# A third buffer for V's global rows, and new written-out orders for all five engines

## The chip, the cores and the metric

The kernel runs on one core of a Trainium2 chip. The time is device microseconds of one execution on that core. Three runs of the kernel before gave 323.43, 324.93 and 328.83 us; their median is 324.93 us.

## The reference

```python
def _attn_ref(q_l, k_l, v_l, q_g, k_g, v_g):          # l: 8 x 8 x 512 x 64, g: 8 x 8 x 32 x 64
    k_all = np.concatenate([k_g, k_l], axis=2); v_all = np.concatenate([v_g, v_l], axis=2)
    out_g = np.matmul(sm(scale * np.matmul(q_g, k_all.T)), v_all)           # global rows see all
    s_ll = np.where(np.abs(pos[:, None] - pos[None, :]) <= 32, scale * q_l @ k_l.T, -1e9)
    s_l = np.concatenate([scale * q_l @ k_g.T, s_ll], axis=-1)              # local rows: 32 global keys and a band
    out_l = np.matmul(sm(s_l), np.concatenate([v_g, v_l], axis=2))
    return np.concatenate([out_g, out_l], axis=2)

def _moe_ref(x, w_in, w_out):                         # x: 4352 x 512, d_ff 2048
    h = x @ w_in
    return (h * np.clip(h + 3.0, 0.0, 6.0) / 6.0) @ w_out
```

Eight batches of eight heads go through a banded attention with 32 global rows; its output, one row of 512 numbers per token, goes through a two-layer network with a hard-swish between the layers. Inputs and output are float32.

## The kernel before

Everything inside is float16 with float32 accumulation. A batch b is cut into four blocks j of 128 local tokens. The work of a batch comes in these steps; the words in italics are used for them below.

- *Loads.* Queries, keys and values come from DRAM in rows of one head, converted to float16 on the way, by DMAs that POOL issues (`load`, the DMA itself at L478): for each block one of queries and one of keys into a buffer `nat` (eight of them, L362), five pieces of values into `ve` (three buffers, one per batch in turn, L366) and the global rows of queries and keys into `natg`. Four small loads per batch put V's global rows, once more, into `vgz` (two buffers before the change, L368): a layout with zeros in which four pairs of heads take 32 rows each (`load_vg`, L559).
- *Turns.* Queries and keys are transposed into `qk`, on TensorE for the first three batches, by DMA transposes that SP issues (L616) for the later ones.
- *Strips.* Two DMAs of SP (L585) copy the values, shifted by half a block, into `st`. They need all five pieces of values of their batch.
- *Score* of (b, j), L676: the products of 64 queries with 128 keys in the band and with the global keys; then the softmax, on VectorE (L701) and ScalarE (L712), and its scaling into `pn` (L731, L737).
- *Turned* (b, j): the weights `pn` transposed into `et`, on TensorE for two batches, later by a DMA transpose of SP (L760).
- *The product with the values* of (b, j): L771 for the global rows out of `vgz`, L776 for the band out of `ve` and `st`. From the seventh block on (`JOIN`, L803) it is emitted together with the score of the block two places later: one operation of TensorE does the score of (2, 2), for instance, and then the value product of (2, 0).
- *Global rows*: their scores (L825), softmax, the transposes (L867 by DMA) and the product with the values (L884, called *gav* below).
- *The network*: `first` (L907, four matmuls of up to 512 columns into one PSUM bank), the activation on ScalarE (L914) and VectorE (L918), `second` (L930), the copy out of PSUM (L399 on ScalarE, L401 on VectorE) and the store by SP (L948).

Each of the five engines does its work strictly in the order of a list, `ORDER` (L16 to L121): the operations' numbers, written out. The lists also say which of ScalarE and VectorE does a copy that either could do. A planner (`Plan.lay`) runs over the lists once when the program is built and gives every operation its buffer; the DMA model in it adds `LATE` (1500 ns) to the landing of a load. When an operation at the head of an engine's list has to wait, all behind it on that engine wait too. That holds for POOL and SP, which only issue DMAs here: 160 on POOL, 114 on SP.

A load waits for what its buffer still holds: one into `nat` for the turn of an earlier block, one into `ve` for all that batch b - 3 does with its values, gav included, and one into `vgz` for the value products of batch b - 2:

```python
deps = [av_last[b - 2, j] for j in range(NJ)] if b >= 2 else [cleared(b)]
```

A DMA besides waits until the one eight places before it on its queue has landed. "Place n" below is the n-th number of an engine's list, counted from 0. Numbers of operations that come up, with what they are: 496 is the last piece of V of batch 2, 497 to 500 are the four vgz loads of batch 2, 735 and 736 the queries and keys of block (3, 0), 985 and 986 those of (4, 3), 1242 the last piece of V of batch 5, 1487 the second piece of V of batch 6; 594 is turned (2, 2), 755 and 756 the turns of (3, 0) and (3, 1), 1008 the turn of (4, 3), 1035 turned (4, 0); 16 is the load of the 32 keys after the first block (the halo, L522).

## Time and profile before

| | |
|---|---|
| three runs | 323.43, 324.93, 328.83 us |
| profiled execution | 326.44 us, of which 324.6 us are the span from first to last instruction |
| busy: TensorE, VectorE, ScalarE, POOL | 307.8, 269.7, 226.2, 121.6 us |
| granted TensorE clock | 1.000 |
| DMA | 46.35 MB in 178864 packets, 169345 of them under 512 B |

Busy time of POOL is the time of issuing DMAs. In the tables of waits an engine's idle time is put down to the instruction after it and to what released that. A DMA's "landing" is counted from its issue to the semaphore that tells of its data. SP's instructions stand as "SPq": they are its queue's own, and their duration is that of the issue, not of the transfer.

### The profile page before, as it was taken

What the parts mean: (1) busy time and instruction counts of PE and PEld (TensorE: products, weight loads), DVE (VectorE), ACT (ScalarE), POOL (GpSimd) and SP (SyncE); (2) the same over time, 40 slices, a digit from 0 to 9 for tenths busy, and PEclk for the clock granted to TensorE, in tenths of its full rate; (3) what the DMA queues carried; (4) which work ended last, traced back from release to release, by engine and by line L of the source; (5) the groups of instructions that cost most, each with busy time, mean ns of one, the idle gap of its engine ahead of it and who ended that gap; (6) DMA issues with size and microseconds to landing.
All of it is one profiled execution on the core that took longest, in us unless ns stands there. A gap on an engine that the chain in (4) does not pass through costs nothing.

```text
span 324.6 us, 9722 instructions
## 1 busy us (share of the span) xinstructions
PE 307.8 (95%) x3653; PEld 174.3 (54%) x3653; DVE 269.7 (83%) x978; ACT 226.2 (70%) x742; POOL 121.6 (37%) x167
## 2 busy tenths in 40 slices
PE   7887989999998999999999779999999999999995
PEld 3566876668854544444544344445444545745543
DVE  4899999899997899799999779999988987476311
ACT  2899999998875797489767566697768664576000
POOL 7966943988820569192208610260000000000000
PEclk9999999999999999999999999999999999999999
DMA  9999999999999999999999998999746027400032
GB/s 153 155 187 177 141 206 164 142 173 142 157 175 205 186 179 158 217 206 142 177 161 182 174 128 205 154 166 146 139 107 162 19 50 107 139 0 2 24 105 98
DMA packets 178864, 46.35 MB, mean 143 GB/s; under 512 B 169345, under 2 KB 173697, under 8 KB 178817
## 3 DMA queue, kind: packets, MB, share of 16 engines
q0 software_dynamic: 108800, 17.28, 75.7%
q1 hardware_dynamic: 70016, 28.45, 47.5%
q8 instruction: 28, 0.46, 0.6%
q14 instruction: 20, 0.16, 0.2%
HBM read 35.65 MB, written 8.91 MB: 137 GB/s over the span
## 4 chain that ended last, share of the span: by engine, by line
PE 55%; DMA 22%; DVE 8%; POOL 7%; issue 3%; SPq 2%; ACT 2%; POOLq 0%; ACTq 0%
PE m L930 24%; PE m L907 23%; DMA et<-pn 9%; DMA wout<-in_moe_w_out_dram 5%; DMA nat<-in_k_l_dram 4%; POOL nat L478 3%; DVE sm L701 2%; DMA nat<-in_q_l_dram 2%; POOL ve L478 2%; SPq L616 2%; PE s L676 2%; PE s L776 2%; DVE pn L731 1%; DMA natg<-in_k_g_dram 1%; PE m L884 1%
## 5 line engine op out<-in xcount | busy, mean ns | idle before, releaser
L712 ACT ACTIVATE sm<-sm,stat 128x160 f32<-128x160 f32 x256 | 106.8, 421 | 28.6 <-DVE stat L701 28.4
L930 PE MATMUL m<-wout,gs 128*128 128x512 f16 (+1 forms) x560 | 125.7, 373 | 0.1
L907 PE MATMUL m<-xt,win 128*128 128x512 f16 (+2 forms) x704 | 119.0, 321 | 0.9 <-ACT xt L399 0.8
L918 DVE SCALAR_TENSOR_TENSOR gs<-t,m 128x512 f16<-128x512 f32 x136 | 89.5, 680 | 13.3 <-ACT t L914 12.8
L907 PEld LDWEIGHTS <-win 128*128 128x128 f16 x768 | 68.7, 98 | 48.6 <-issue 1.6
L914 ACT ACTIVATE t<-m 128x512 f32<-128x512 f32 x136 | 77.5, 594 | 24.6 <-PE m L907 22.6
L930 PEld LDWEIGHTS <-gs 128*128 128x128 f16 x560 | 52.8, 98 | 56.2 <-issue 1.6
L701 DVE CUSTOM_DVE_ANT_0 sm<-s,mask 128x160 f32<-128x160 f32 x256 | 69.1, 317 | 7.4 <-PE s L776 4.5
L712 ACT ACTIVATION_READ_ACCUMULATOR sm<-sm,stat 128x1 f32 x256 | 49.0, 192 | 0.0
L731 DVE TENSOR_TENSOR pn<-sm,stat 128x512 f16<-128x512 f32 x64 | 43.3, 685 | 0.6
L478 POOL DMA_DIRECT2D ve<-in_v_l_dram x40 | 32.7, 827 | 25.6 <-PE m L884 17.7
L478 POOL DMA_DIRECT2D nat<-in_q_l_dram x30 | 27.2, 907 | 15.2 <-DMA qk<-nat 9.9
L399 ACT COPY ot<-m 128x512 f32<-128x512 f32 (+1 forms) x22 | 12.2, 561 | 25.7 <-PE m L930 24.6
L478 POOL DMA_DIRECT2D vgz<-in_v_g_dram x28 | 15.8, 570 | 37.0 <-PE s L771 35.6
L478 POOL DMA_DIRECT2D nat<-in_k_l_dram x30 | 27.0, 905 | 5.9 <-DMA ve<-in_v_l_dram 2.7
L676 PEld LDWEIGHTS <-qk 64*64 64x64 f16 x1024 | 13.8, 107 | 15.8 <-issue 13.3
L401 DVE COPY ot<-m 128x512 f32<-128x512 f32 x13 | 9.0, 689 | 15.7 <-PE m L930 15.7
L701 DVE DVE_READ_ACCUMULATOR2_ANT stat<- 128x1 f32 x256 | 21.0, 82 | 0.0
L676 PE MATMUL s<-qk 64*64 64x128 f16 x512 | 17.1, 224 | 3.7 <-DVE stat L701 1.8
L401 DVE CAST xt<-s 128x512 f16<-128x512 f32 x26 | 17.8, 684 | 2.6 <-PE s L776 2.6
L676 PE MATMUL s<-gt,qk 64*64 64x32 f16 x512 | 14.7, 176 | 0.0
L737 DVE TENSOR_TENSOR pn<-sm,stat 128x256 f16<-128x256 f32 x32 | 13.4, 419 | 0.2
(82 smaller groups left out, 242.9 us busy)
## 6 DMA issues: line engine op xcount, KB each, us to landing
out_dram<-ot SPq DMA_DIRECT2D x31, 256.0 KB, 4.2
nat<-in_q_l_dram POOLq DMA_DIRECT2D x30, 128.0 KB, 6.4
nat<-in_k_l_dram POOLq DMA_DIRECT2D x30, 128.0 KB, 7.3
st<-ve SPq DMA_DIRECT2D x14, 256.0 KB, 4.5
ve<-in_v_l_dram POOLq DMA_DIRECT2D x24, 128.0 KB, 5.9
win<-in_moe_w_in_dram POOLq DMA_DIRECT2D x4, 512.0 KB, 8.7
wout<-in_moe_w_out_dram POOLq DMA_DIRECT2D x4, 512.0 KB, 11.4
ve<-in_v_l_dram POOLq DMA_DIRECT2D x8, 96.0 KB, 5.6
```

Of the source, the lines that this page charges most:

```text
L399: nc.scalar.copy(out=out, in_=in_)
L401: nc.vector.tensor_copy(out=out, in_=in_)
L478: nc.gpsimd.dma_start(out=dst(op), in_=src)
L676: nc.tensor.matmul(out=out[q, P:KW] if n == G else out[q, 0:P], lhsT=qk[r][rows, 0, p, UQ + j * P + u * QP:UQ + j * P + (u + 1) * QP], rhs ...
L701: nc.vector.tensor_tensor_reduce(out=sm[sm_op.slot][:, h, :], in0=head(psS[s.slot], h), in1=m, scale=-scale, scalar=3.0e38, op0=ALU.add, o ...
L712: nc.scalar.activation(out=sm[sm_op.slot][:, h, :], in_=sm[sm_op.slot][:, h, :], func=EXP, scale=-1.0, bias=stat[stat_op.slot][:, 0, h:h + 1],
L731: nc.vector.tensor_tensor(out=pn[pn_op.slot][:, h0:h1, :], in0=sm[sm_op.slot][:, h0:h1, 0:P], in1=stat[stat_op.slot][:, 2, h0:h1].unsqueez ...
L737: nc.vector.tensor_tensor(out=pn[pn_op.slot][:, H:H + 2, :].rearrange("q a (h g) -> q (a h) g", g=G), in0=sm[sm_op.slot][:, :, P:KW], in1= ...
L907: nc.tensor.matmul(out=psM[op.slot][:, i * n:(i + 1) * n], lhsT=w_in_t[:, m, (c + i) * P:(c + i + 1) * P], rhs=x()[:, m, t0:t0 + n], start ...
L914: nc.scalar.activation(out=t1[to.slot], in_=psM[f.slot], func=RELU, bias=0.5, scale=1.0 / 6.0)
L918: nc.vector.scalar_tensor_tensor(out=gs[set_.slot][:, c:c + k, t0:t0 + n], in0=t1[to.slot].rearrange("f (k t) -> f k t", k=k), scalar=1.0, ...
L930: nc.tensor.matmul(out=psM[(f or op).slot][:, a * n:(a + 1) * n], lhsT=gs[set_.slot][:, c, t0:t0 + P], rhs=w_out_t[:, c, a * n:(a + 1) * n ...
```

## The change

`vgz` becomes three buffers, used in turn; its loads wait for the value products of batch b - 3 in place of b - 2; the second clearing step sets one more buffer to zero; and all five lists of `ORDER` are replaced.

```diff
-    vgz = many(2, [P, NP, P], FP16, "vgz")
+    vgz = many(3, [P, NP, P], FP16, "vgz")
...
-            nc.vector.memset(vgz[r], 0.0)
+        for x in vgz[:1] if first else vgz[1:]:
+            nc.vector.memset(x, 0.0)
...
-    add("DVE", 1100, lambda: clear(False), key=-5.0)
+    add("DVE", 1640, lambda: clear(False), key=-5.0)
...
-        deps = [av_last[b - 2, j] for j in range(NJ)] if b >= 2 else [cleared(b)]
+        deps = [av_last[b - 3, j] for j in range(NJ)] if b >= 3 else [cleared(b)]
...
-        return [load(lambda op, k=k: vgz[b % 2]...
+        return [load(lambda op, k=k: vgz[b % 3]...
...
-    lhsT=vgz[r][...]
+    lhsT=vgz[b % 3][...]
```

TensorE's list holds the same 372 operations in both; 140 of them stand at the same place, and no block's score moves by more than a few places (the score of (2, 2) is at place 93 in both, that of (4, 2) at 170 in both). The score of (3, 0) goes from 115 to 116, gav of batch 3 from 185 to 189. Ten copies go from VectorE to ScalarE and six the other way. The lists of POOL and SP hold the same DMAs in another order. POOL's, places 37 to 161:

```diff
     "POOL": """
...
-        226 224 228 221 222 45 481 229 230 46 47 48 482 487 479 480 483 488 489 490 485 496 484 492 497 486 495
-        493 494 491 739 747 1229 745 741 987 499 737 500 498 738 988 981 742 989 735 750 736 751 752 990 1725
-        1231 743 749 744 740 1232 979 982 980 746 748 1241 983 1240 1239 995 999 993 998 984 997 994 1235 1230
-        985 1238 1236 992 1481 996 986 1479 991 1246 1243 1244 1000 1475 1727 1476 1726 1482 1237 1484 1723 1245
-        1242 1233 1234 1729 1488 1483 1492 1477 1473 1724 1728 1494 1474 1489 1487 1491 1493 1480 1730 1490 1478
-        1485 1486 1737 1736 1740 1735 1733 1731 1739 1738 1732 1734
+        227 221 222 231 47 230 229 232 45 46 48 481 482 487 490 479 480 483 488 489 484 494 485 745 486 492 495
+        737 493 491 738 735 739 741 747 742 1229 496 497 987 990 499 989 500 498 988 751 981 750 744 740 982 748
+        736 985 746 749 979 980 1725 991 743 752 1231 1242 993 983 1235 1239 1479 996 984 1238 1237 1230 995
+        1241 994 1233 1000 1236 998 1245 1481 997 992 999 1234 986 1473 1240 1232 1723 1474 1475 1476 1487 1729
+        1486 1730 1243 1244 1724 1480 1246 1727 1477 1740 1488 1737 1489 1478 1483 1482 1484 1490 1738 1732 1734
+        1493 1728 1736 1739 1494 1485 1731 1733 1726 1735 1491 1492
```

And the first lines of SP's:

```diff
     "SP": """
-        11 16 10 19 20 234 233 457 502 501 539 756 566 755 594 471 478 464 758 757 621 1006 753 754 785 734 1005
-        812 720 840 1007 867 727 713 1002 1008 1035 1001 978 964 1250 1062 876 883 1249 1090 1247 1252 1251 1117
+        11 19 10 16 20 233 234 457 539 501 502 758 478 566 755 756 594 757 1006 621 471 734 753 754 785 1005 720
+        812 840 464 1007 867 713 727 1001 1002 1008 1035 978 964 1248 1062 1250 1249 876 883 1090 1247 957 1251
```

## The prediction

> **What bounds the kernel now.** I read the page first, then the table of waits, POOL's timeline, the chain of waits, and SP's timeline beside TensorE's.

> ```profile
> PE 307.8 (95%) x3653; PEld 174.3 (54%) x3653; DVE 269.7 (83%) x978; ACT 226.2 (70%) x742; POOL 121.6 (37%) x167
> ```

> TensorE is busy for 307.8 of 324.6 us, and the change takes no matmul away. What can be won is its idle time; what can be lost is more of it. So the question about each of the other engines is only whether it lets TensorE wait.

> ```profile
> POOL vgz L478 <- PE s L771: 35.6, 3, 19.7
> ...
> POOL ve L478 <- PE m L884: 17.7, 1, 17.7
> ...
> PE s L771 <- DMA et<-pn: 3.4, 3, 2.5
> ...
> PE s L676 <- DVE stat L701: 1.8, 3, 0.8
> ```

> The columns are the total in us, the number of times and the longest. POOL stands for 35.6 us in front of loads into vgz, three times, until a value product of two batches earlier is done. That is the wait which the third buffer takes away. TensorE, however, waits only 3.4 us for transposed weights and 1.8 us for VectorE's softmax in these rows. The wait on POOL is seven times what reaches TensorE. The timeline of POOL tells where the three are, and what is queued behind each:

> ```profile
> 109.03 0.89 POOL L478 DMA_DIRECT2D ve<-in_v_l_dram  x1 [17.68 <-PE m L884]
> ...
> 136.82 2.15 POOL L478 DMA_DIRECT2D vgz<-in_v_g_dram  x4 [7.38 <-PE s L771]
> ...
> 171.45 0.54 POOL L478 DMA_DIRECT2D vgz<-in_v_g_dram  x1 [8.55 <-PE s L771]
> ...
> 209.16 0.53 POOL L478 DMA_DIRECT2D vgz<-in_v_g_dram  x1 [19.72 <-PE s L771]
> ...
> 214.21 1.71 POOL L478 DMA_DIRECT2D ve<-in_v_l_dram  x2
> ```

> ```profile
> 228.71 0.56 SPq L585 DMA_DIRECT2D st<-ve  x1
> ```

> Behind the longest of them (19.72 us) only batch 7's values and vgz rows are left; the last is issued by 215.9, and SP's copy of them into the strips starts at 228.71. A margin of 12.8 us against a landing of some 6 us (row of the vgz loads below) says that this wait costs nothing. The one that ends at 136.82 holds the vgz rows of batch 4 and loads of batches 5 to 7, none of which TensorE is seen to wait for. Only the one that ends at 171.45 stands near a stall:

> ```profile
> 159.71 0.58 PE m L884 x20
> ...
> 172.17 8.47 DMA et<-pn
> ```

> ```profile
> 180.68 0.31 PE L771 MATMUL s<-et,vgz 64*64 64x128 f16 x8 [2.53 <-DMA et<-pn]
> ...
> 188.32 0.74 PE L884 MATMUL m<-eg,ve 128*128 128x64 f16 x20 [1.68 <-DVE gs L918]
> ```

> The chain runs through the transpose of weights (5, 0) issued at 172.17, which takes 8.47 us. It was issued 0.7 us after POOL came free and began to issue a dozen loads without a pause. TensorE idles 2.53 us for it, and 1.68 us more 7 us later, when ScalarE and VectorE have to catch up. How much of the 8.47 us is POOL's doing is seen in all transposes of weights, from 60 to 200 us and after 200, when few loads are left:

> ```profile
> L760 SPq DMA_TRANSPOSE et<-pn x15: 1336/2433/3948, 70.4 to 193.7; - x15
> ...
> DMA to landing us min/median/max: 3.4/7.2/9.4
> ```

> ```profile
> L760 SPq DMA_TRANSPOSE et<-pn x9: 1255/1339/1898, 201.6 to 275.8; - x9
> ...
> DMA to landing us min/median/max: 3.4/3.4/5.0
> ```

> The same transpose lands after 7.2 us beside loads and after 3.4 us without. A load that goes out early is therefore not free: it lengthens the transpose beside it, on which TensorE's value products wait.

> **The change part by part.** The sum is made against the profiled execution: 326.44 us, span 324.6 us and 1.84 us around it. It lies 1.5 us above the median of 324.93 us of three runs from 323.43 to 328.83, so it is one ordinary run. The numbers of instructions on POOL, SP and TensorE stay what they are.

> *The clear and the halo.* One more memset of vgz:

> ```profile
> 2.59 0.27 DVE L450 MEMSET vgz<- 128x256 uint32 x1
> ...
> 6.53 0.22 DVE L401 COPY gt<-m 128x128 f16<-128x128 f16 x1 [2.16 <-PE m L641]
> ```

> It costs VectorE 0.27 us at a time after which it idles 2.16 us for TensorE; hidden, and 0.27 us if that cover were gone. On SP the halo load goes from place 1 to place 3, past the loads 19 and 10 (both of 256 KB).

> ```profile
> 1.27 0.56 SPq L522 DMA_DIRECT2D t<-in_k_l_dram  x1
> ```

> ```profile
> single<-in_q_l_dram SPq DMA_DIRECT2D x2, 256.0 KB, 5.1
> ...
> t<-in_k_l_dram SPq DMA_DIRECT2D x1, 64.0 KB, 2.7
> ```

> ```profile
> 7.48 1.08 ACT qk L399 x2
> 8.60 0.57 PE s L676 x32
> ```

> Behind two more issues like its own of 0.56 us it goes out at about 2.4. It lands at 5.1 if it takes its 2.7 us again, at 7.5 if it takes the 5.1 us of the big ones ahead of it. Then come four small transposes and a copy like that of 0.22 us above. The first score starts at 8.60 behind ScalarE's copies, which end at 8.56: that is the cover. I take 0; bounds 0 and +0.5. Copies that change between ScalarE and VectorE I take at 0: in the middle TensorE waits for none of them, and the last copy before the last store stays on ScalarE (0.37 us below is all that it could add).

> ```profile
> 321.04 0.37 ACT L399 COPY ot<-m 128x256 f32<-128x256 f32 x1 [2.66 <-PE m L930]
> ```

> *Batch 2's loads go back.* In POOL's list 496 moves from place 52 to 68 and the vgz loads 497 to 500 from 55, 70, 67 and 69 to 69, 75, 72 and 74, behind loads of batch 3. TensorE's operation that uses them keeps its place.

> ```profile
> 76.06 0.58 POOL L478 DMA_DIRECT2D natg<-in_q_g_dram  x1
> ```

> ```profile
> 79.33 0.28 PE L771 MATMUL s<-et,vgz 64*64 64x128 f16 x8
> ```

> ```profile
> L478 POOL DMA_DIRECT2D vgz<-in_v_g_dram x28: 533/552/762, 24.6 to 213.7; - x28
> ...
> DMA to landing us min/median/max: 3.3/5.9/9.9
> ```

> Place 75 was issued at 76.06 before; a vgz load there lands at 82.0 by the median, 2.6 us after its use at 79.33. But the places 68 to 75 now hold small loads that issue in some 0.55 us (the median of that row), where four were full loads of about 0.9 us (0.89 in the row at 109.03): up to 1.4 us earlier, so 1.2 us late. I take **+1.5 us**, near that end, since the eight places before it are all small now; bounds 0 (a landing after 3.3 us) and +6.6 us (after 9.9).

> *Batch 3's turns.* The keys 736 of block (3, 0) move from place 78 to 84, and turned (2, 2) now stands behind both turns of batch 3 (place 16, was 14).

> ```profile
> 78.27 6.16 DMA nat<-in_k_l_dram
> ```

> ```profile
> 82.55 0.62 POOL L478 DMA_DIRECT2D ve<-in_v_g_dram  x1
> ```

> ```profile
> 84.47 1.24 SPq L616 DMA_TRANSPOSE qk<-nat  x1
> ...
> 89.20 1.47 SPq L760 DMA_TRANSPOSE et<-pn  x1
> ```

> ```profile
> 96.99 0.28 PE L771 MATMUL s<-et,vgz 64*64 64x128 f16 x7
> ```

> The load at 78.27 took 6.16 us and let SP go at 84.47. At place 84 it is issued at 82.55 and lands at 88.7; two turns of 1.24 us follow, and turned (2, 2) goes out at 91.2 in place of 89.20. Its weights land 7.2 us later, at 98.4; the value product wants them at 96.99, so 1.4 us late. As TensorE is itself already up to 1.5 us behind by then, but part of this lag moves the transpose too, I take **+1.0 us**, bounds 0 and +2.5.

> *Behind the wait for gav 2.* POOL's wait of 17.68 us for ve stays where it is: place 95 (1242) wants gav of batch 2 as place 94 did. Behind it the keys 986 of block (4, 3) stand at place 119, were at 113.

> ```profile
> 127.08 0.90 POOL L478 DMA_DIRECT2D nat<-in_k_l_dram  x1
> ```

> ```profile
> 133.83 2.00 SPq L616 DMA_TRANSPOSE qk<-nat  x1
> 136.07 2.43 SPq L760 DMA_TRANSPOSE et<-pn  x1
> ```

> ```profile
> 146.40 0.28 PE L771 MATMUL s<-et,vgz 64*64 64x128 f16 x8
> ```

> From 109.03 to 127.08 are 19 places, 0.95 us each. 24 places give 131.8; the landing took 6.75 us (127.08 to 133.83), so SP's turn goes out at 138.6, turned (4, 0) 2.2 us behind it at 140.8, and its weights land at 148.0, 1.6 us after 146.40. I take **+1.3 us** since some small loads are among the 24; bounds 0 and +3.8 (a landing of 9.4 us).

> *The wait that goes, and the one that comes.* No vgz load stands any more in front of what is urgent. But 1487, a piece of V for batch 6, now stands at place 127 and wants gav of batch 3, done at 160.3. From 109.03 the 32 places before it take 30 us, so POOL comes to it at 139 and waits there for about 20 us, where it had stood for 7.38 and 8.55 us. When it is let go at 160, the loads behind it run beside the weights of (4, 2) and (4, 3) in place of (5, 0). The stall of 2.53 and 1.68 us may go; some of it comes back there. I take **-1.5 us**; bounds -4.2 and 0.

> [...]

> The sum: 326.44 + 0 + 1.5 + 1.0 + 1.3 - 1.5 = **328.7 us**, 1.2% over the median. Two per cent of it, 6.5 us, is about what a measurement of this kernel can tell from no change: 318.4 to 331.4 us.

> **The rivals.** *The stalls go and nothing comes.* The chain through 172.17 speaks for it: POOL free earlier, loads spread out, no burst beside (5, 0). TensorE gets back 2.53 + 1.68 us and the other 0.9 us of its 3.4 us for weights: 326.44 - 5.1 = 321.3 us. Against it are the ve waits, which hold POOL as long as the vgz waits did, and the places of 496 to 500. With VectorE's 1.8 us besides it would be 319.5, which is about the floor.

> *SP's line gets late in every batch: slower.* Turns and weights share SP's list, so a late load of keys holds a turn, and that holds the weights behind it. It decides where the keys at places 84 and 119 land over 6.2 and 6.75 us after their issue; from then each late us goes to TensorE. At the longest landings seen the first batch costs 6.6 us and the fourth 3.8: 326.44 + 10.4 = 336.8 us. For it: landings of 9.4 and 9.9 us are in the rows, and three value products already wait for weights. Against it: a lag of TensorE gives later loads time again.

> *A wait for a wait.* The ve wait does what the vgz wait did, moved batches cancel out: the change does not do what it says, and the time stays at 326.4 us, as the profiled run, or 325 by the median.

> **How the numbers follow.** Forecast 0.37, its own range 325.5 to 332.5; the stalls go 0.20; SP's line late 0.33; a wait for a wait 0.10. Faster by over 2% takes the lower two fifths of the second: 0.08. Slower by over 2% takes all of the third and 0.05 of the forecast: 0.38. Within 2%: 0.54. The range from 319.5 to 338 runs from the floor of the second case to just over the third's price.

> **What would show it.** Right: POOL's waits for vgz near 0 and one wait for ve of 15 to 20 us that ends near 160; a wait of TensorE for vgz or st near 79 and for et near 97 and 146; less at 178 to 188. Wrong: no wait of TensorE over 1 us between 75 and 150 (then the places of 496, 736 and 986 were priced too high), or waits for et over 2 us in several batches (then SP's line decides).

## The result, and the profile after

The kernel after takes 322.57 us (median of 22 executions, 318.55 to 328.94), the kernel before beside it on the same chip 326.86 us (22 executions, 321.81 to 331.34). The ratio is 0.9892 [0.9855, 0.993]: 1.1% faster, with the executions of the two overlapping. Ratios here are taken over those executions that lie within 1.5% of their kernel's fastest (13 of the 22 of after); the two medians alone would give 0.987. The profiled execution of after takes 322.16 us, its span 320.4 us.

First the page, engines' busy time, then the tables of waits of TensorE and POOL (total us, times, longest; lines from L451 on are one higher than before):

```profile
PE 308.5 (96%) x3658; PEld 174.4 (54%) x3658; DVE 266.4 (83%) x975; ACT 229.5 (72%) x746; POOL 121.4 (38%) x167
```

```profile
PE s L772 <- DMA et<-pn: 2.4, 3, 1.6
...
PE s L777 <- DMA st<-ve: 0.5, 1, 0.5
...
POOL ve L479 <- PE m L885: 23.3, 3, 12.2
POOL nat L479 <- DMA qk<-nat: 23.0, 4, 9.7
```

TensorE's work is the same. The 35.6 us for which POOL stood in front of loads into vgz are gone, and about half of them come back in other places: 23.3 us for gav in front of loads into ve (17.7 before) and 23.0 us for turns in front of loads into nat (9.9 before). POOL issues its last load at 194.6 us, where it was 215.9. What TensorE loses, by its timeline:

```profile
79.31 0.32 PE L777 MATMUL s<-et,st 128*64 128x64 f16 x8 [0.48 <-DMA st<-ve]
...
88.74 0.31 PE L772 MATMUL s<-et,vgz 64*64 64x128 f16 x8 [1.57 <-DMA et<-pn]
...
99.59 0.31 PE L772 MATMUL s<-et,vgz 64*64 64x128 f16 x8 [0.26 <-DMA et<-pn]
...
121.89 0.31 PE L772 MATMUL s<-et,vgz 64*64 64x128 f16 x8 [0.52 <-DMA et<-pn]
```

The chain of waits names the transfers behind the first two of these, a piece of V, the strips and turned (2,1):

```profile
69.00 6.93 DMA ve<-in_v_l_dram
...
75.96 3.22 DMA st<-ve
...
79.26 9.44 DMA et<-pn
```

There are new waits early, as the prediction had it, though only one of them is over 1 us, and none is left where the kernel before lost 2.53 and 1.68 us. TensorE's busy time in two stretches, before and then after (columns: window, its length, TensorE, its weight loads, VectorE, ScalarE, POOL, granted clock, DMA share, GB/s):

```profile
160.00:180.00 20.00, 18.12 (x239) 8.76 (x235) 18.81 (x67) 13.33 (x49) 10.30 (x14) 1.00 1.48 174
180.00:200.00 20.00, 17.64 (x192) 8.75 (x195) 15.92 (x57) 14.39 (x47) 4.98 (x7) 1.00 1.62 175
```

```profile
160.00:180.00 20.00, 19.86 (x277) 9.89 (x276) 17.61 (x65) 12.88 (x47) 14.45 (x20) 1.00 1.79 195
180.00:200.00 20.00, 20.00 (x216) 9.95 (x214) 19.81 (x76) 15.88 (x53) 10.47 (x16) 1.00 1.79 161
```

35.76 us of work in 40 before, 39.85 after: 4.1 us, nearly the whole difference of 4.3 us between the two profiled executions. It is tempting to stop here. The experiments show that the place of this gain belongs in part to these two executions and not to the kernels.

### The profile page after: what moved, and what is told of

Read it like the earlier page. It is cut to its first block, busy times and chain, and to the rows that moved or that the text cites. A ratio compares the mean times of both kernels' runs of the same rounds, so it can differ in the third digit from the quotient of the medians.

```text
span 320.4 us, 9717 instructions
## 1 busy us (share of the span) xinstructions
PE 308.5 (96%) x3658; PEld 174.4 (54%) x3658; DVE 266.4 (83%) x975; ACT 229.5 (72%) x746; POOL 121.4 (38%) x167
## 4 chain that ended last, share of the span: by engine, by line
PE 67%; DVE 15%; DMA 14%; issue 2%; ACT 1%; POOL 1%; POOLq 0%
PE m L931 33%; PE m L908 23%; DMA et<-pn 9%; DVE sm L702 4%; DVE gs L919 4%; DVE pn L732 3%; PE s L677 3%; PE s L777 3%; DMA ve<-in_v_l_dram 2%; DMA natg<-in_k_g_dram 1%; PE m L885 1%; PE s L772 1%; DMA st<-ve 1%; ACT sm L713 1%; PE m L749 1%
## 5 line engine op out<-in xcount | busy, mean ns | idle before, releaser
L479 POOL DMA_DIRECT2D ve<-in_v_l_dram x40 | 33.1, 833 | 27.1 <-PE m L885 23.3
L399 ACT COPY ot<-m 128x512 f32<-128x512 f32 (+1 forms) x28 | 15.8, 573 | 16.3 <-PE m L931 14.8
L401 DVE CAST xt<-s 128x512 f16<-128x512 f32 x26 | 17.8, 685 | 1.5 <-PE s L777 1.4
L841 DVE TENSOR_REDUCE stat<-s 128x1 f32<-128x544 f32 x16 | 11.4, 714 | 3.1 <-PE s L826 2.8
L1059 PE MATMUL m<-idle 128*128 128x512 f16 x44 | 12.6, 415 | 1.2 <-DVE idle L443 1.2
## 6 DMA issues: line engine op xcount, KB each, us to landing
out_dram<-ot SPq DMA_DIRECT2D x31, 256.0 KB, 3.2
st<-ve SPq DMA_DIRECT2D x14, 256.0 KB, 5.2
wout<-in_moe_w_out_dram POOLq DMA_DIRECT2D x4, 512.0 KB, 10.4
```

The lines of the kernel that those rows point to most:

```text
L399: nc.scalar.copy(out=out, in_=in_)
L401: nc.vector.tensor_copy(out=out, in_=in_)
L479: nc.gpsimd.dma_start(out=dst(op), in_=src)
L1059: order = plan.fill(plan.lay(av_last[1, 0]), lambda ring, i: lambda: nc.tensor.matmul(out=spare[ring][i], lhsT=idle[:, 0:P], rhs=idle))
```

## The experiments

The first four ask which part of the change makes the gain. **Theory T**: the buffer. **Theory L**: the lists. In the kernels made for these runs the lists fill fewer lines, so most line numbers are 89 lower than in the kernel that each was made from (L683 in the run of the buffer alone is L772 of after); in the runs with small loads they are 4 higher.

*The buffer alone.* After, with the five lists of before.

```diff
-ORDER = (the five lists of after)
+ORDER = (the five lists of before)
```

> The third vgz buffer with the five old lists. Theory T (the buffer itself): POOL no longer stands 8.55 us before 171, its loads for batch 6 go out from 163 on instead of in a burst beside the transpose of weights (5, 0), TensorE's waits of 2.53 and 1.68 us between 177 and 189 shrink to under 1 us together, and the ratio to before is about 0.988. Theory L (the lists): POOL's 35.6 us for vgz go, but other loads at the same places take the same burst to the same transpose; the ratio is 0.996 to 1.004 and waits of 2 us or more remain between 170 and 190.

Measured: 328.31 us (12 executions; before beside it 327.31), ratio 1.0077 [1.0004, 1.015]. Its waits:

```profile
PE s L683 <- DMA et<-pn: 2.5, 4, 1.5
PE s L588 <- DMA qk<-nat: 2.0, 1, 2.0
...
POOL nat L390 <- DMA qk<-nat: 21.6, 4, 7.7
POOL ve L390 <- PE m L796: 20.4, 2, 19.5
```

POOL's wait for the value products is away, others come instead, and nothing is won. Between 170 and 190 us TensorE waits once, 1.5 us at 183.8, less than L said, and the ratio lies a little above L's (the two medians give 1.003, inside it). 35.6 us of a waiting POOL were worth nothing by themselves.

*The lists alone, with two buffers.* The lists of after would wait for themselves with two buffers, so the four vgz loads of batch 7 go to the end of POOL's list.

```diff
-vgz = many(3, ...)                      (and b % 3, b - 3)
+vgz = many(2, ...)                      (and b % 2, b - 2)
 POOL: 1740, 1737, 1738, 1739 moved to the end
```

> The five new lists with two vgz buffers; the four vgz loads of batch 7 are put at the end of POOL's list. Theory L: POOL waits 15 us or more for vgz again, TensorE waits under 1.5 us between 170 and 190, and the ratio is 0.985 to 0.993. Theory T: the waits for vgz hold the loads behind them as before, TensorE waits 3 us or more in all behind them, and the ratio is 0.998 to 1.01.

Measured: 332.96 us, ratio 1.0286 [1.0159, 1.0412].

```profile
PE s L587 <- DMA qk<-nat: 5.0, 1, 5.0
...
POOL vgz L389 <- PE s L682: 22.0, 2, 12.5
```

With two buffers the wait for vgz, 12.5 us up to 139.3, stands in front of a load of keys, which goes out at 143.4 and lands after 5.96 us; its turn comes late, and a score waits 5.0 us for it. In this form, with four loads moved, the lists lose without the third buffer.

*Two mixtures, three buffers each*: POOL's list new with the other four old, and POOL's old with the other four new.

```diff
 e4: ORDER of before, but "POOL" of after
 e5: ORDER of after, but "POOL" of before
```

> Three vgz buffers, POOL's list new, the other four old. If the gain is in the places of the loads alone: ratio 0.985 to 0.993 and no stall at 177 to 189. If it takes the lists of SP and the compute engines that go with it: ratio 1.0 or above, since SP's old list asks for loads in another order than POOL's new one brings them; waits of TensorE for transposes of 3 us or more somewhere from 75 to 150.

> Three vgz buffers, POOL's list old, the other four new. If the gain is in the lists of SP and the compute engines: ratio 0.985 to 0.993. If it is in the places of the loads: ratio 0.997 to 1.01, with the stall at 177 to 189 there again.

Measured: 333.4 us, ratio 1.0306 [1.0212, 1.0401], and 334.73 us, ratio 1.0328 [1.022, 1.0435]. TensorE's longest waits in the first, then in the second:

```profile
PE s L683 <- DMA et<-pn: 6.3, 4, 4.7
```

```profile
PE s L683 <- DMA et<-pn: 9.3, 5, 4.2
PE m L538 <- DMA nat<-in_k_l_dram: 1.8, 1, 1.8
```

The first came out as its second reading had it, with the longest wait at 80 to 85 us; the second missed both of its readings. No part of the change gains anything when it is tried alone: the four cost 0.8 to 3.3% by the ratios, 0.3 to 2.3% by the medians. T and L both fall as stated.

The next four look at the stall at 178 to 189 us. Turned (5,0) goes out 1.5 us earlier after the change (170.70, was 172.17) and lands 2.4 us faster (6.07, was 8.47). **Theory S**: SP's order, since before it a turn and two stores stand ahead of it. **Theory B**: the loads that POOL lets loose beside it.

*S alone.* Before, with the turn (6,1) and two stores behind turned (5,0).

```diff
-SP: ... 1248 1500 971 957 1279 1221 ...
+SP: ... 1248 1279 1500 971 957 1221 ...
```

> Question: why TensorE no longer stalls at 178 to 189 us. In the kernel before, SP issues the turn (6,1) and the last half of two stores (168.72 to 172.08) ahead of turned (5,0), which goes out at 172.17 and lands at 180.64; after the change they stand behind it, and it goes out at 170.70 and lands at 176.77. This kernel is the kernel before with only those three SP operations (1500, 971, 957) moved behind turned (5,0). Theory S (SP's order): turned (5,0) goes out near 170.6, its landing is 1.5 us or more earlier, the stall of 2.5 us falls to 1 us or less, and the time falls by 1 to 2.5 us (ratio 0.992 to 0.997). Theory B (the loads beside it): it still goes out into the dozen loads that POOL begins at 171.5, lands after 8 us or more, the stall stays over 1.5 us, and the 1.8 us before the global value product stays.

Measured: 331.15 us (before beside it 326.23, here and in the next three), ratio 1.0205 [1.0114, 1.0297]; both theories missed. Turned (5,0) went out at 174.88, for TensorE was 4 us late at (5,0) already, before the place of the edit; it landed after 4.82 us. The chain of waits in its execution:

```profile
178.62 5.31 DMA out_dram<-ot
183.94 0.02 issue
183.96 0.70 DVE ot L312
184.66 0.04 issue
184.70 3.57 PE m L818 x8
```

A store was not as free as it looked: it holds an output buffer `ot`, VectorE's next copy waits for that buffer, and TensorE for the copy, 4.67 us. The granted clock in this stretch of the execution (the third number from the end):

```profile
181.00:182.00 1.00, 0.00 (x0) 0.00 (x0) 0.00 (x0) 0.00 (x0) 1.00 (x3) 1.00 1.54 218
182.00:183.00 1.00, 0.00 (x0) 0.00 (x0) 0.00 (x0) 0.00 (x0) 1.00 (x2) 0.80 1.96 235
183.00:184.00 1.00, 0.00 (x0) 0.00 (x0) 0.04 (x1) 0.00 (x0) 0.89 (x2) 0.50 1.65 273
...
188.00:189.00 1.00, 1.00 (x41) 0.80 (x40) 0.20 (x2) 0.69 (x2) 1.00 (x3) 0.50 1.59 253
189.00:190.00 1.00, 1.00 (x32) 0.65 (x23) 0.86 (x2) 0.39 (x1) 0.53 (x1) 0.79 1.60 159
```

*B alone.* Before, with the load 1492, for which POOL stands until 171.45, behind the loads queued after it.

```diff
-POOL: ... 1483 1492 1477 1473 ... 1487 1491 1493 ...
+POOL: ... 1483 1477 1473 ... 1487 1492 1491 1493 ...
```

> The kernel before with one load moved in POOL's list: the first vgz load of batch 6 (1492), for which POOL stands still until 171.45 us, goes behind the loads queued after it, to just ahead of 1491. Two buffers stay. Theory B (POOL held, then a dozen loads beside turned (5,0)): the loads go out from 163 on, the transposes of 172 to 190 land after 5 to 6 us in place of 8 to 10, the stalls of 2.5 and 1.8 us go, and the time falls by 2.5 to 4 us (ratio 0.987 to 0.993). Theory S (SP's order): turned (5,0) still goes out behind the turn (6,1) and two stores near 172, and at least 1.5 us of stall stays; ratio 0.996 to 1.003. Rival that the lists are tuned to each other: the loads now meet turned (4,3) and turned (5,0) both, and a new stall of 1 us or more stands at 165 to 175; ratio 1.00 to 1.02.

Measured: 328.27 us, ratio 1.0122 [1.0041, 1.0204]. Turned (5,0) went out at 170.75 and landed after 9.48 us; TensorE still waited 2.1 us. The ratio is the one of the third reading, but the 2.1 us stand at 180.3, where the stall stood before. The loads went earlier, and the transposes met them all the same. Here, moving the wait moved the traffic and did not take it away.

*Both moves* (`SP` and `POOL` as in the two diffs above).

> The kernel before with both moves: the three SP operations behind turned (5,0), and the vgz load 1492 later in POOL's list; two buffers, compute lists untouched. If the whole gain of the change is in the stall at 178 to 189 us and S and B each carry part of it, this has none of the 2.5 and 1.8 us and takes 322 to 324 us where the kernel before takes 326.5 (ratio 0.987 to 0.992), without a third buffer. If the gain needs the buffer or the new compute lists: ratio 0.997 or more, with a stall of over 1.5 us at some other place.

Measured: 332.89 us, ratio 1.0203 [1.0088, 1.0318], with the store's wait again, longer:

```profile
PE m L818 <- DVE ot L312: 7.8, 1, 7.8
```

*The wait put back into after.*

```diff
-POOL: ... 1476 1487 1729 1486 ... 1488 1737 1489 ...
+POOL: ... 1476 1737 1487 1729 1486 ... 1488 1489 ...
```

> The kernel after with one load moved up in POOL's list: a vgz load of batch 7 (1737) goes from behind 1488 to in front of 1487, so that POOL stands still again until a value product of batch 4 near 171 us, as it did before the change, and begins the dozen loads behind it beside turned (5,0). Theory B: turned (5,0) or the two transposes of the global weights behind it land after 8 us or more, and TensorE stalls again by 2 to 4 us between 175 and 190; time 1 to 1.3% over the kernel after (ratio to before 0.998 to 1.003). Theory S: SP's list is that of the kernel after, so turned (5,0) goes out at 170.7 and TensorE has no stall over 1 us there; ratio 0.986 to 0.993.

Measured: 331.37 us, ratio 1.0245 [1.0185, 1.0305]. This does not decide between S and B, for the wait held back other loads than I had meant:

```profile
PE s L683 <- DMA et<-pn: 4.9, 4, 1.7
PE s L683 <- DMA vgz<-in_v_g_dram: 4.6, 2, 3.3
```

Vgz rows of batch 5 stood behind it, and turned (5,0) landed after 4.4 us. It does show that such a wait ahead of urgent loads costs: 331.37 us, where the kernel after took 322.57.

*The traffic itself.* Before, with twelve of the loads of 171.45 to 189 us cut to 16 of their rows.

```diff
+            if op.n in SMALL:       # 12 loads of batches 6 and 7
+                nc.gpsimd.dma_start(out=dst(op)[0:16], in_=src[0:16])
```

> What the loads beside SP's transposes cost, measured by itself. The kernel before, all five lists and two buffers as they are; twelve of the loads that POOL issues from 171.45 to 189 us (pieces of queries, keys and values of batches 6 and 7) move only the first 16 of their rows and leave the other rows of those buffers unfilled, so the arithmetic of batches 6 and 7 runs on other data in the same time. Every instruction, wait and semaphore stays. Theory B (traffic): turned (5,0), which lands after 8.5 us, lands after 3.5 to 5 us, the two transposes of the global weights after 4 to 6 in place of 8 to 10, the stalls of 2.7 and 1.8 us near 178 and 187 go, and the time falls by 3.5 to 5 us (ratio 0.984 to 0.990). Theory S (order of SP and of the stores, not traffic): turned (5,0) still goes out at 172 and TensorE still loses 1.5 us or more there; ratio 0.994 or more.

Measured: 324.5 us (319.27 to 326.49; before beside it 327.09), ratio 0.9856 [0.9773, 0.9938]. Landings of the global weights' transposes from 171 to 190 us, in the kernel before and then here:

```profile
DMA to landing us min/median/max: 8.1/9.0/9.8
```

```profile
DMA to landing us min/median/max: 4.0/4.2/4.3
```

Here TensorE loses nothing between 170 and 190, with two buffers and all old lists:

```profile
170.00:190.00 20.00, 20.00 (x219) 9.92 (x214) 18.84 (x67) 16.47 (x59) 8.99 (x17) 1.00 1.17 169
```

Turned (5,0) went out at 174.3 there, later than the 172.17 of before, and landed after 5.5 us, a little over what B said; an earlier place on SP's list, S, is not needed. For the global weights B is shown: in the twelve profiles with whole loads the same two transposes take 5.0 us or more, 24 times out of 24. For the stall of 2.53 us it is argued. In this run turned (5,0) went out 0.1 us before POOL came free, so it had none of the dozen loads ahead of it, small or whole. So it was in the run of S alone (out at 174.88, POOL free at 175.53, landed after 4.82 us) and in the next one (171.42, 172.10, 4.71 us), both with whole loads; in the first profile of before it went out 0.7 us after POOL came free. Which of the two goes first is decided by less than a microsecond.

*Each kernel once more*, unchanged.

> The kernel before as it is, one more execution with a profile. If the stalls of 2.7 and 1.8 us at 178 to 189 belong to its lists, they are there again, within 1 us in size and place. If they were an accident of that one execution, they are under 1 us together, and stalls of 1 to 2 us stand elsewhere between 60 and 200 us.

> The kernel after as it is, one more execution with a profile. If its lists keep the place at 175 to 190 us free, TensorE loses under 1 us there again, and 1.5 to 2 us near 87 us, where the weights of (2,1) came late. If the first profile was lucky, there is a stall of 1 us or more at 175 to 190 us or elsewhere after 100 us.

Measured: 323.99 us and 323.81 us. What is left of the stalls, in the second execution of before and then of after (TensorE's timeline):

```profile
185.80 0.74 PE L884 MATMUL m<-eg,ve 128*128 128x64 f16 x20 [1.20 <-DVE gs L918]
```

```profile
88.88 0.31 PE L772 MATMUL s<-et,vgz 64*64 64x128 f16 x8 [1.62 <-DMA et<-pn]
...
172.52 0.31 PE L772 MATMUL s<-et,vgz 64*64 64x128 f16 x8 [2.17 <-DMA et<-pn]
```

In this execution of before turned (5,0) landed after 4.71 us in place of 8.47, and its 2.53 us are not there; two waits for weights of 1.25 and 1.21 us stand at 121 and 137 us instead, so neither reading of that run holds in full. After has a stall of 2.17 us that it did not have. The stall before gav of batch 4 comes again (1.20, was 1.68): there the second transpose of the global weights lands just before the product starts (188.19 and 188.32 in the first profile, 185.66 and 185.80 in this), so the DMA ends that wait and not VectorE, whom the row names. The wait near 88.8 in after also comes again. The start of some scores on TensorE, in us, shows how far executions of the same lists differ (the kernels of the rows marked + differ from before only later than this):

```
                      (2,2)   (3,0)   (4,0)   (4,2)   (5,0)   (6,0)
before                78.96   96.62  129.08  146.02  161.95  199.78
before, again         78.95   96.61  128.85  146.65  162.60  197.26
+ small loads late    79.94   97.88  132.16  148.77  164.96
+ 1492 later          78.74   96.40  127.57  145.54  161.20
+ SP moved            79.21  100.58  133.10  150.27  166.03
+ both moves          79.70   97.35  131.33  149.41  165.07
after                 77.92   98.80  130.37  145.92  162.17  195.77
after, again          78.69   98.94  129.94  145.49  161.58  197.04
```

The same lists reach (5,0) between 161.2 and 166.0 us. A single pair of profiles cannot account for 4 us. This left open whether the new lists are shorter or only stand up better to late transfers. **Theory C**: the second. **Theory D**: the compute order itself is shorter.

*Both kernels with small loads.* All 70 loads of queries, keys and values of batches 3 to 7 cut to 16 rows.

```diff
+            if op.n in SMALL:       # 70 loads of batches 3 to 7
+                nc.gpsimd.dma_start(out=dst(op)[0:16], in_=src[0:16])
```

> The kernel before, its five lists and two buffers as they are; the 70 loads of POOL that bring queries, keys and values of batches 3 to 7 move only the first 16 of their rows and leave the rest of those buffers unfilled, so batches 3 to 7 compute on other data in the same time. The small loads of global rows stay whole. Theory C (how the lists stand up to late transfers): most of what TensorE loses after 75 us is landings beside loads, so this takes 318 to 321 us (ratio to the kernel before 0.974 to 0.983), no wait of TensorE over 1 us stands after 75 us, and the granted clock stays at 1. Theory D (the compute order itself is better after the change): the lists before keep a loss of 2 us or more after 75 us that no transfer makes, and this takes 322 us or more.

> The kernel after, with its third buffer and new lists; the same 70 loads move only the first 16 of their rows. Theory C: without the traffic there is nothing left for which the new lists are better, and this takes the same as the kernel before with small loads, within 1 us. Theory D: it is 2.5 us or more faster than that one, as after is faster than before with whole loads.

Measured: before 319.25 us (318.6 to 321.51), ratio 0.9827 [0.9767, 0.9888]; after 318.27 us (317.68 to 318.38), ratio 0.9785 [0.974, 0.983], both against the whole kernel before. In neither profile is a wait of TensorE listed between 60 and 200 us, and the clock is 1.00 in both. Landings of the transposes of weights from 60 to 200 us, before with small loads and then after with small loads:

```profile
DMA to landing us min/median/max: 3.4/3.9/5.9
```

```profile
DMA to landing us min/median/max: 3.3/3.8/6.5
```

and POOL's waits in the first:

```profile
POOL vgz L482 <- PE s L775: 48.6, 3, 24.3
POOL ve L480 <- PE m L888: 27.4, 2, 22.7
```

Of the 4.3 us between the medians, 1.0 us is left when the traffic is thin. The kernel before pays 7.5 us for its transfers (326.78, measured beside, to 319.25), the kernel after 4.3 us (322.57 to 318.27, not measured beside each other; the medians of the kernel before lie between 326.23 and 327.31 in all five sets). By the ratios in place of the medians it is 1.4 us of 3.5. C holds for six to eight tenths of the gain, D for the rest. POOL waits 48.6 us for vgz there, more than the 35.6 of before, in an execution of 319.3 us: the wait that gave the change its reason is not what the time was lost to. (The small loads also take POOL less issuing, 99.7 us of busy time for 121.6; the runs do not part that from the bytes.)

## Why the prediction was wrong, point by point

It said 328.7 us, slower by 1.2% than the median; it is 322.6. The likeliest case was the wrong one, and the first rival's 321.3 us was nearest.

- *The step that failed: late landings as fixed costs of the new lists.* The sum took each landing of one profiled execution as a fixed number and asked for each moved step whether it comes 1 or 2 us late. Its terms for transfers come to +2.3 us (+3.8 and -1.5). Measured with whole and with small loads, transfers cost the kernel before 7.5 us and the kernel after 4.3 us: -3.2 us by the medians, about -2 by the ratios, and the order itself, put at 0, adds another -1.0 to -1.4. The executions of the same lists in the table above are 4.8 us apart at (5,0) alone, twice the sum's +2.3. What the change does lies in how much a late landing costs TensorE, in either kernel, and no term was of that kind. The prediction's own range, 325.5 to 332.5 us, is not worked out in it: the bounds of its terms add up to 322.2 to 339.8.
- *Clear, halo, copies, 0.* They hide, but the other order of copies and turns up to there was not worth 0: (2,2) starts 1.04, 0.26 and, with small loads (79.37 and 78.50), 0.87 us earlier. That is about the size of Theory D's part.
- *Batch 2's loads, +1.5.* Place 75 was issued at 74.46, a little before the 74.7 that the term assumed (0.28 us after the landing of the load eight DMAs before it, for which POOL had stood for 1.40 us), and landed after 2.97 us, not 5.9: its rows came in time; what came late was 496, the piece of V, and by it the strips: 0.48 us. Right in kind, three times too large.
- *Batch 3's turns, +1.0.* (3,0) starts 2.2 us and 2.3 us later than before in the two pairs. With small loads it starts 0.1 us earlier, so the loss is one of transfers. It is real and larger than the term, by another step: turned (2,1) landed after 9.4 us (79.26 to 88.70), and TensorE waited 1.57 us at 88.74. Turned (2,2), which the term was about, went out at 93.36 and cost 0.26 us.
- *Places of 986, +1.3.* No wait near 146 came; at (4,2) after is 0.1 and 1.2 us ahead. What was lost at (3,0) was given back by then, 2.3 and 3.5 us of it. With small loads the new order gains 0.9 us on the same stretch, and the kernel before has stalls of its own there (0.89 and 0.49 us near 105 in its first profile, which the prediction left uncosted, 1.25 and 1.21 us in its second); the rest is open:

```profile
104.38 0.25 PE L676 MATMUL s<-qk 64*64 64x128 f16 x3 [0.89 <-DMA qk<-nat]
...
105.39 0.31 PE L771 MATMUL s<-et,vgz 64*64 64x128 f16 x8 [0.49 <-DMA et<-pn]
```

A lag of TensorE that covers the next late load was named in the prediction, against the rival of SP's line, and went into the sum only where batch 3's turns were taken at +1.0.
- *The wait that goes and the one that comes, -1.5.* POOL's wait for gav 3 ended at 164.42 after 6.92 us, not at 160 after 20, since loads into nat had held it for 8.18 and 9.69 us on the way. From (5,0) to (6,0) before takes 37.8 and 34.7 us, after 33.6 and 35.5: -4.2 in one pair, +0.8 in the other; with small loads 33.3 and 33.0. The cause named, loads beside SP's transposes, is borne out by the runs with small loads. That the moved wait spreads them is not shown: after issues loads without a pause from 164.42 to 178 us, beside turned (5,0) as well, and moving only that wait (1492 later) left the stall. The 1.68 us were put down to ScalarE and VectorE, as the row has it; it was the transpose.
- *The rivals.* "The stalls go and nothing comes" had the size but not the reason. SP's line did get late at 88 us in both executions of after, once and not in every batch. "A wait for a wait" described POOL in part: of the 35.6 us 5.6 came back in front of ve and 13.1 in front of nat; only POOL's waits do not set the time. The prediction's own signs settle neither way: one wait of TensorE over 1 us came between 75 and 150, at 88.74, and none near 146.

Not settled: which of the moves in the lists make them bear late transfers better. The two-buffer run speaks for the buffer being needed, but it moved four loads as well; and POOL's list of one kernel with the other four of the other is worse than either kernel.

## What to carry to other kernels

Where orders are written out by hand and transfers land when they can, a kernel has a time with thin traffic and a price for the traffic (here 319.25 and 7.5 us before, 318.27 and 4.3 us after); measure both, by cutting the bytes of the loads and leaving every instruction, before reading anything into one profile. Profile the unchanged kernel twice: a stall that is not there the second time, as the 2.53 us before the value product of (5,0) were not, is a chance, not a place. And the wait of an engine that only issues loads is no cost until one names the load behind it that comes late (in the kernel before with small loads POOL waits 48.6 us for vgz, in an execution of 319.3 us); what such a list can win is slack at the places where landings scatter most, and here it won it only as a whole: three operations of SP moved by one place were enough to hold an output buffer and through it TensorE for 4.67 us.

## What the runs showed of the hardware

*Transposes landed later beside loads in flight.* In the twelve profiles with whole loads there are 284 transposes of weights by SP after 60 us. From issue to landing they take 3.6 us by the median with no load of POOL in flight at their issue (123 of them), 5.0 with one (18), 6.1 with two or three (35) and 7.5 with four or more (108; a tenth of these over 10.0). That the loads are the cause is borne out by the runs with small loads, 7.2 us to 3.9 by the median from 60 to 200 us.

*The stall of 4.67 us had a second price.* In the run of S alone above, TensorE stands still from 180.03 to 184.70, and the granted clock is 0.50 from 182.6 to 189.4. Eight matmuls of `first` take 3.57 us there, twenty of them 4.48 us from 190.53 on, at a clock of 1.00: 0.446 and 0.224 us for one. So the 4.7 us of work at half the clock are an estimated 2.4 us more on top of the 4.67. The two-buffer run shows the same after its 5.0 us:

```profile
148.00:153.00 5.00, 0.79 (x4) 0.20 (x3) 1.50 (x5) 0.71 (x3) 0.00 (x0) 1.00 1.79 180
153.00:160.00 7.00, 5.89 (x66) 2.85 (x66) 3.08 (x16) 2.97 (x9) 1.75 (x2) 0.51 1.17 218
```

The stalls of 2.53 us in before and 2.17 in the second execution of after lowered nothing, but after two of 2.00 and 0.49 us in the run of the buffer alone the clock was halved, and after one of 1.93 us in the run of S alone. In these runs the length of a stall does not decide it. In all fifteen profiles the stretches of one clock, but for the last, which ends with the profile, take whole multiples of 3.41 us: the full clock 320.85 us in before (94 of them, from 4.99 us on) and 317.44 us in after (93, from 3.83 us on), the half clock 6.8 us in the run of S alone (182.6 to 189.4). Two stretches of 3.41 us in turn of the run of S alone, with the stall of 1.93 us in the first of them, and then three of before, counted from 4.99 us on, where a border at 179.07 cuts the 2.53 us in two:

```profile
87.03:90.44 3.41, 1.48 (x62) 1.06 (x60) 3.00 (x7) 1.02 (x3) 2.92 (x4) 1.00 2.84 147
90.44:93.85 3.41, 3.41 (x16) 2.02 (x15) 3.26 (x18) 1.00 (x3) 3.41 (x5) 0.50 1.67 136
```

```profile
175.65:179.07 3.42, 2.50 (x42) 1.15 (x41) 3.35 (x10) 2.82 (x10) 3.42 (x5) 1.00 2.00 164
179.07:182.48 3.41, 1.80 (x30) 1.07 (x30) 1.84 (x11) 0.12 (x1) 1.76 (x4) 1.00 2.02 202
182.48:185.89 3.41, 3.41 (x18) 1.52 (x17) 2.85 (x11) 3.41 (x12) 2.21 (x3) 1.00 2.21 141
```

So late transfers cost more than their sum in these runs: 4.67 us and an estimated 2.4 in the run of S alone. The mean granted clock of whole executions shows it too: it is at least 0.999 in 16 of 22 of after (median 322.4 us; the other six 326.9), and in 20 of 51 of before (325.7; the other 31 327.6). It is 0.995 or less in 4 of the 22 and in 27 of the 51; 3.41 us at half the clock in a span of 322 us make 0.995. At 0.999 or more the two are 3.3 us apart, and the kernel after is halved more seldom.
